# The MLP's transposed rows and relu rows begin at other places within 256 bytes of SBUF

## The chip, the cores and the metric

One core of one Trainium2 chip. The metric is the device time of one execution in microseconds (us); lower is better. A change under 0.2% (about 2.1 us) can't be told from no change with runs of this kernel.

## The reference

Attention with random features (FAVOR), then layer normalisation and an MLP with a residual. Batch 8, 8 heads, 576 positions, head width 64, 128 features; the MLP is 512 -> 2048 -> 512, over 8 * 576 = 4608 rows, all in float32.

```python
q_s, k_s = q * scale, k * scale            # scale = 1 / sqrt(sqrt(64))
def phi(x):
    h = x @ omega.T - sum(x * x) / 2
    return exp(h - max(h)) / sqrt(m)
q_p, k_p = phi(q_s), phi(k_s)
num = q_p @ (k_p.T @ v);  den = q_p @ sum(k_p) + 1e-06
x   = num / den                            # to 8 x 576 x 512
xn  = (x - mean) / sqrt(var + 1e-06) * g_ln
out = x + relu(xn @ w_ch1) @ w_ch2
```

## The kernel before

The 4608 rows of the MLP are cut into nine tiles `t` of T = 512 rows, and the 2048 inner columns into 16 slices `f` of 128. A planner (`Plan`) runs all parts of the work as generators and writes down, in the order in which they come due by its costs, the instructions of each engine; what it fixes is an order for each engine, not times. The MLP's matmuls (`gen_mlp`) are the work of lowest rank that is always there: they stand in the TensorE's order in a fixed sequence, mm1(t, f) and then mm2 of the slice before, and the attention's small matmuls (L480, L510, L582, L583, L671, L755) are put between them where they come due.

Every product of the MLP is made of three matmuls in the type float32r (a float32 that the array takes in one pass at less precision), since each factor is split in a high part and the low part that remains: high by high, low weights by high rows, high weights by low rows.

- `gen_xnT1` (L755 to L761): four 128x128 transposes of one 128-row piece of the normalised rows go to a PSUM bank. ScalarE copies the bank to the high part of the tile `xnT` (L759), VectorE writes the rest to the low part (L761). `xnT` is one tile of 128 partitions x (2 parts, NK = 4 pieces of the inner dimension, 512 rows); there is one buffer of it.
- `mm1` (L782 to L784): for each of the four pieces k, the weights `w` of w_ch1 (128 columns of them) are the stationary operand and the 512 elements of row `xnT[:, part, k]` are the moving operand. The sum stands in a PSUM bank `b`.
- `relu` (L793, L795): ScalarE writes the high part of relu to the tile `hid`, VectorE the low part; `hid` is 128 partitions x (2 parts, 512), in two buffers, hid0 and hid1.
- `mm2` (L815 to L817): for each of four groups of 128 rows, 128 elements of `hid` are the stationary operand and 512 elements of the weights of w_ch2 the moving one. They add up over the 16 slices in four PSUM banks.

So `xnT` is read by matmuls (moving) and `hid` by weight loads (stationary, LDWEIGHTS). The weights `w1`, `w2` stay in SBUF for the whole run, 4096 bytes in each partition for a slice: 512 high, then 512 low elements.

In the built program all tiles of weights, `xnT`, both `hid`, `wide`, `kp` and `x` begin at a multiple of 256 bytes within a partition, and each row of 512 elements is 2048 bytes long. So every row that a matmul of the MLP streams, and every group of 128 elements that it loads as weights, begins at byte 0 of 256. The attention's `v` tiles don't: they have 65 elements for each head (260 bytes), and the three buffers begin at byte 128 (v0), 32 (v1) and 96 (v2) of 256.

Of the kernel before, what the change touches and what calls it, by code (L numbers as in the profile page):

```python
# [14 lines left out]
F32R = mybir.dt.float32r  # L15
U32 = mybir.dt.uint32
AF = mybir.ActivationFunctionType
ALU = mybir.AluOpType
# [4 lines left out]
P = 128  # L23
# [5 lines left out]
NK = DM // P  # L29
NF = DFF // P  # L30
# [5 lines left out]
T = 512  # L36
# [32 lines left out]
class Plan:  # L69
# [73 lines left out]
    def free(self, *names):  # L143
        for n in names:
            assert n not in self.places, n
            self.places[n] = self.cur.seen()
            self.cur.holds -= n[0] == "b" and 0 < self.cur.holds
            self.wake(lambda w: w[0] == "get" and n in w[1])

    def done(self, key):  # L150
        self.made[key] = self.cur.seen()
        self.wake(lambda w: w == ("wait", key))
# [38 lines left out]
def favor_ffn(ctx, tc, kT, kTr, vF, vR, qT, qD, omT, gT, w1, w2, out):  # L191
# [12 lines left out]
    nc = tc.nc  # L204
# [8 lines left out]
    def f32(ap):  # L213
        return ap.bitcast(F32)

    def act(n, k=1, c=0.09):
        return "run", {ACT: k * (c + 0.00084 * n)}

    def dve(n, k=1, c=0.065):
        return "run", {DVE: k * (c + 0.00105 * n)}  # L220

    def us(eng, t):
        return "run", {eng: t}
# [16 lines left out]
    def wait(*key):  # L240
        return "wait", key

    def names(tag, n):
        return plan.own(*(f"{tag}{i}" for i in range(n)))

    def tile_of(tag, shape, dtype=F32, pool=None):
        pool = pool or (wp if tag[1].isdigit() and tag[0] == "w" else small if tag[0:2] in ("kv", "mb", "st") or tag[0] == "v" else sb)
        return pool.tile(shape, dtype, tag=tag, name=tag, bufs=1)
# [6 lines left out]
    def bank(tag, n=512):  # L255
        return tile_of(tag, [P, 512], F32, ps)[:, 0:n]
# [5 lines left out]
    n_hid, n_xnT, n_mb, n_st = names("hid", 2), names("xnT", 1), names("mb", 3), names("st", 6)  # L262
# [6 lines left out]
    def at_now():  # L269
        return b_at if mlp_on else banks  # L270
# [118 lines left out]
    kvs, phis, xs, xnTs, pvs, pvt = {}, {}, {}, {}, {}, {}  # L389
# [341 lines left out]
    def gen_xnT():  # L731
        for c in range(NC):
            t, i = divmod(c, TC)
            plan.cur.rank = URGENT + t
            yield wait("x", c)
            xn_turn = yield "get", turn["xn"]
            t_n = yield "get", n_big
            _, x, mu, rs = xs[c]
            xn = tile_of(t_n, [P, DM])
            yield us(DVE, 0.34)  # L740
            nc.vector.tensor_scalar(out=xn, in0=x, scalar1=mu, scalar2=rs, op0=ALU.subtract, op1=ALU.mult)
            done(("xn", c))
            if i == 0:
                t_t = yield "get", n_xnT
                xnTs[t] = t_t, tile_of(t_t, [P, 2, NK, T], F32R)
            plan.add(plan.cur.rank, gen_xnT1(t, i, xn, t_n, xn_turn))

    def gen_xnT1(t, i, xn, t_n, xn_turn):
        xnT = xnTs[t][1]
        yield wait("ident")  # L750
        t_b = yield "get", at_now()
        yield us(PE, 0.46)
        pt = bank(t_b).rearrange("p (a b) -> p a b", b=P)
        for k in range(NK):
            nc.tensor.transpose(pt[:, k], xn[:, k * P : (k + 1) * P], ident)  # L755
        free(t_n, xn_turn)
        cols = slice(i * P, (i + 1) * P)
        yield us(ACT, 0.5)
        nc.scalar.copy(out=xnT[:, 0, :, cols], in_=pt)  # L759
        yield dve(DM)  # L760
        nc.vector.tensor_tensor(out=xnT[:, 1, :, cols], in0=pt, in1=f32(xnT[:, 0, :, cols]), op=ALU.subtract)  # L761
        free(t_b)
        done(("xnT", t, i))

# [3 lines left out]
    def mm1(t, f):  # L768
        for k in range(NK):
            yield wait("w", 1, f // NK * NK + k)  # L770
        for i in range(TC):
            yield wait("xnT", t, i)
        if not mlp_on:
            mlp_on.append(True)
        t_x, xnT = xnTs[t]
        t_b = yield "get", b_h
        ph = bank(t_b)
        for k in range(NK):
            yield us(PE, 3 * 0.225)
            w = wparts[1, f // NK * NK + k]  # L780
            cs = slice(f % NK * P, (f % NK + 1) * P)
            nc.tensor.matmul(ph, w[:, 0, cs], xnT[:, 0, k], start=(k == 0), stop=False)  # L782
            nc.tensor.matmul(ph, w[:, 1, cs], xnT[:, 0, k], start=False, stop=False)  # L783
            nc.tensor.matmul(ph, w[:, 0, cs], xnT[:, 1, k], start=False, stop=(k == NK - 1))  # L784
        if f == NF - 1:
            free(t_x)
        plan.add(MOST_URGENT, relu(t, f, t_b, ph))

    def relu(t, f, t_b, ph):
        t_h = yield "get", n_hid  # L790
        hl = tile_of(t_h, [P, 2, T], F32R)
        yield act(T, 1, 0.05)
        nc.scalar.activation(out=hl[:, 0], in_=ph, func=AF.Relu)  # L793
        yield dve(T)
        nc.vector.scalar_tensor_tensor(  # L795
            out=hl[:, 1], in0=ph, scalar=0.0, in1=f32(hl[:, 0]), op0=ALU.max, op1=ALU.subtract
        )
        free(t_b)
        hid[t, f] = t_h, hl
        done(("hid", t, f))  # L800

    accs = {}

    def mm2(t, f):
        yield wait("w", 2, f)
        yield wait("hid", t, f)
        t_h, hl = hid[t, f]
        w = wparts[2, f]
        for i in range(TC):
            if f == 0:  # L810
                t_b = yield "get", (b_acc[i],)
                accs[i] = bank(t_b)
            yield us(PE, 3 * 0.225)
            cs = slice(i * P, (i + 1) * P)
            nc.tensor.matmul(accs[i], hl[:, 0, cs], w[:, 0], start=(f == 0), stop=False)  # L815
            nc.tensor.matmul(accs[i], hl[:, 0, cs], w[:, 1], start=False, stop=False)  # L816
            nc.tensor.matmul(accs[i], hl[:, 1, cs], w[:, 0], start=False, stop=(f == NF - 1))  # L817
            if f == NF - 1:
                plan.add(MOST_URGENT, result(t, i, accs[i]))
        free(t_h)  # L820

    def result(t, i, acc):
        c = t * TC + i
        t_x, x = xs[c][0:2]
        yield dve(DM)
        nc.vector.tensor_tensor(out=x, in0=acc, in1=x, op=ALU.add)  # L826
        free(b_acc[i])
        yield dma(P * DM)
        nc.sync.dma_start(out[c * P : (c + 1) * P], x)
        free(t_x)  # L830
# [11 lines left out]
    def gen_mlp():  # L842
        last = None
        for t in range(NT):
            for f in range(NF):
                if f == 0 and last:
                    yield from mm2(*last)
                    last = None
                yield from mm1(t, f)
                if last:  # L850
                    yield from mm2(*last)
                last = t, f
        yield from mm2(*last)
# [14 lines left out]
    plan.add(RK, gen_keys())  # L868
    plan.add(RQ, gen_queries())
    plan.add(URGENT, gen_xnT())  # L870
    for b in range(B):
        plan.add(0, gen_kvfree(b))
# [54 lines left out]
```

## Time and profile before

| | |
|---|---|
| median of three runs | 1043.0 us (1042.22 to 1043.11) |
| the profiled execution: span from first to last instruction | 1040.8 us |
| the profiled execution's own device time | not given apart from the span; the span is 2.2 us under the median of the runs |
| granted TensorE clock | 1.000 |
| TensorE matmul, busy | 1032.0 us (99%), 5778 instructions |
| weight loads, busy | 863.4 us (83%) |
| VectorE / ScalarE / GpSimd, busy | 498.3 (48%) / 357.1 (34%) / 133.5 us (13%) |
| MLP matmuls (L782 to L784, L815 to L817) | 6 x 576 = 3456 |

A matmul's busy time in the profile is the time from its start to its modelled end, and neighbours overlap in the array: how fast the array takes matmuls is read from the distance between two starts, not from the mean duration. "PEld" is the weight load, which runs beside the matmul before it.

### The profile page before, as it was taken

Reading aid. Unit: us, or ns where it says so; the run is one execution under the profiler, and the core shown is the slowest. Engines: PE = TensorE matmul, PEld = TensorE weight load, DVE = VectorE, ACT = ScalarE, POOL = GpSimd, SP = SyncE. Lnnn points to the kernel's source line nnn. Section 1 sums busy time; section 2 is a strip of 40 time slices with the busy share of each in tenths; the row PEclk is TensorE's granted clock in tenths of the full one; section 3 lists DMA queues with packets and bytes.
Section 4 is the critical chain, followed back from the end, with each engine's and each line's share of the span. In section 5 each row is a group of like instructions: output and inputs, shape, how many; then the busy total and the mean of one; then the engine's idle time right before and its main releaser. Section 6 shows DMA issues by size and latency. Waiting matters only on the chain.

```text
span 1040.8 us, 14483 instructions
## 1 busy us (share of the span) xinstructions
PE 1032.0 (99%) x5778; PEld 863.4 (83%) x5778; DVE 498.3 (48%) x1045; ACT 357.1 (34%) x810; POOL 133.5 (13%) x80
## 2 busy tenths in 40 slices
PE   9999999999999999999999999999999999999998
PEld 7888888888887888888887888888878888888886
DVE  6999878366347521663147422751274134113112
ACT  7699746335334421253025421241133111102100
POOL 6000424014002300050002200140022000000000
PEclk9999999999999999999999999999999999999999
DMA  9564222121213100420032100200030010001001
GB/s 358 213 195 150 82 82 91 62 72 51 73 43 130 42 11 1 143 61 1 1 99 85 41 1 1 102 21 1 1 122 1 0 41 1 1 1 42 1 1 41
DMA packets 30308, 64.08 MB, mean 62 GB/s; under 512 B 3488, under 2 KB 3616, under 8 KB 30240
## 3 DMA queue, kind: packets, MB, share of 16 engines
q1 hardware_dynamic: 30240, 63.14, 17.9%
q8 instruction: 46, 0.75, 0.3%
q14 instruction: 22, 0.18, 0.1%
HBM read 53.69 MB, written 9.44 MB: 61 GB/s over the span
## 4 chain that ended last, share of the span: by engine, by line
PE 93%; DVE 4%; DMA 2%; SPq 1%; issue 1%; ACT 0%; ACTq 0%
PE b L815 13%; PE b L782 13%; PE b L784 12%; PE b L817 12%; PE b L816 12%; PE b L783 12%; PE b L480 5%; PE b L671 5%; PE b L510 3%; PE b L582 1%; PE b L583 1%; PE b L755 1%; DMA w<-w 1%; DVE x L826 1%; DMA w<-vF 0%
## 5 line engine op out<-in xcount | busy, mean ns | idle before, releaser
L795 DVE SCALAR_TENSOR_TENSOR hid<-b,hid 128x512 fp32r<-128x512 f32 x144 | 99.3, 689 | 382.5 <-ACT hid L793 381.9
L793 ACT ACTIVATE hid<-b 128x512 fp32r<-128x512 f32 x144 | 86.3, 599 | 445.8 <-PE b L784 445.4
L815 PE MATMUL b<-w,hid 128*128 128x512 f32 x576 | 231.6, 402 | 0.0
L782 PE MATMUL b<-xnT,w 128*128 128x512 f32 x576 | 230.4, 400 | 0.0
L817 PE MATMUL b<-w,hid 128*128 128x512 f32 x576 | 225.2, 391 | 0.0
L784 PE MATMUL b<-xnT,w 128*128 128x512 f32 x576 | 225.0, 391 | 0.1
L816 PE MATMUL b<-w,hid 128*128 128x512 f32 x576 | 224.9, 390 | 0.0
L783 PE MATMUL b<-xnT,w 128*128 128x512 f32 x576 | 224.5, 390 | 0.0
L604 POOL PARTITION_ALL_REDUCE wide<-wide x72 | 132.4, 1877 | 658.2 <-ACT st L713 268.3
L784 PEld LDWEIGHTS b<-xnT,w 128*128 128x128 f32 x576 | 108.2, 188 | 23.6 <-DVE xnT L761 0.5
L817 PEld LDWEIGHTS b<-w,hid 128*128 128x128 f32 x576 | 108.2, 188 | 23.0
L815 PEld LDWEIGHTS b<-w,hid 128*128 128x128 f32 x576 | 108.4, 188 | 22.6
L782 PEld LDWEIGHTS b<-xnT,w 128*128 128x128 f32 x576 | 108.4, 188 | 21.8
L783 PEld LDWEIGHTS b<-xnT,w 128*128 128x128 f32 x576 | 108.4, 188 | 20.6
L816 PEld LDWEIGHTS b<-w,hid 128*128 128x128 f32 x576 | 108.5, 188 | 20.3
L448 ACT ACTIVATE kp<-b,mb 128x128 f32<-128x128 f32 x272 | 75.3, 388 | 51.4 <-DVE mb L442 51.4
L671 PEld LDWEIGHTS b<-kv,wide 128*128 128x128 f32 (+1 forms) x640 | 67.2, 181 | 6.9 <-issue 2.8
L607 DVE TENSOR_TENSOR wide<-wide,wide 128x512 f32<-128x512 f32 x72 | 65.1, 909 | 13.3 <-POOL wide L604 12.8
L480 PEld LDWEIGHTS b<-v,kp 128*128 128x128 f32 (+1 forms) x576 | 64.2, 191 | 6.5 <-issue 1.6
L671 PE MATMUL b<-kv,wide 128*128 128x65 f32 (+1 forms) x640 | 66.8, 261 | 2.3 <-DVE st L678 1.2
L480 PE MATMUL b<-v,kp 128*128 128x65 f32 (+1 forms) x576 | 64.0, 272 | 0.0
L442 DVE TENSOR_REDUCE mb<-b 128x4 f32<-128x512 f32 x72 | 46.6, 681 | 30.9 <-PE b L510 30.8
(71 smaller groups left out, 800.0 us busy)
## 6 DMA issues: line engine op xcount, KB each, us to landing
w<-w SPq DMA_DIRECT2D x32, 512.0 KB, 8.9
wide<-qD SPq DMA_DIRECT2D x64, 256.0 KB, 2.7
out<-x SPq DMA_DIRECT2D x36, 256.0 KB, 2.0
v<-vF SPq DMA_DIRECT2D x28, 260.0 KB, 2.9
wide<-kT SPq DMA_DIRECT2D x28, 256.0 KB, 2.7
w<-vF SPq DMA_DIRECT2D x4, 260.0 KB, 4.8
v<-vR SPq DMA_DIRECT2D x4, 260.0 KB, 4.0
w<-kT SPq DMA_DIRECT2D x4, 256.0 KB, 4.8
```

What stands on the lines that cost most here:

```text
L448: nc.scalar.activation(out=kp[:, j], in_=pk[:, i], func=AF.Exp, scale=1.0, bias=mb[:, j : j + 1])
L480: nc.tensor.matmul(o[:, i], kp[r, slot(h)], v[r, h], start=(n > 0 or c + i == 0), stop=(n > 0 or (c == NFULL and i == 3)),)
L604: nc.gpsimd.partition_all_reduce(mx, qc, P, bass_isa.ReduceOp.max)
L671: nc.tensor.matmul(pn[a:z, i], phi(blk, h, slice(cols + a, cols + z)), kvs[b][1][:, h], start=True, stop=True)
L782: nc.tensor.matmul(ph, w[:, 0, cs], xnT[:, 0, k], start=(k == 0), stop=False)
L783: nc.tensor.matmul(ph, w[:, 1, cs], xnT[:, 0, k], start=False, stop=False)
L784: nc.tensor.matmul(ph, w[:, 0, cs], xnT[:, 1, k], start=False, stop=(k == NK - 1))
L793: nc.scalar.activation(out=hl[:, 0], in_=ph, func=AF.Relu)
L795: nc.vector.scalar_tensor_tensor(out=hl[:, 1], in0=ph, scalar=0.0, in1=f32(hl[:, 0]), op0=ALU.max, op1=ALU.subtract)
L815: nc.tensor.matmul(accs[i], hl[:, 0, cs], w[:, 0], start=(f == 0), stop=False)
L816: nc.tensor.matmul(accs[i], hl[:, 0, cs], w[:, 1], start=False, stop=False)
L817: nc.tensor.matmul(accs[i], hl[:, 1, cs], w[:, 0], start=False, stop=(f == NF - 1))
```

## The change

The tiles `xnT`, `hid0` and `hid1` become 64 elements (256 bytes) longer, and their rows are laid with gaps: a high row of `xnT` every 516 elements, a low row every 520, after the high ones; the two rows of `hid` begin at elements 8 and 528 in hid0, at 32 and 560 in hid1. All instructions stay the same in kind, number, order, size and waits on every engine: the two programs' orders differ in source lines alone. Since three tiles are longer by 256 bytes, the tiles that lie behind them in SBUF move by 256, 512 or 768 bytes; all keep their place within 256. The weights don't move at all.

The places at which rows begin, in bytes within 256, by the built programs:

| rows | read as | before | after |
|---|---|---|---|
| `xnT` high, k = 0, 1, 2, 3 | moving (L782, L783) | 0, 0, 0, 0 | 0, 16, 32, 48 |
| `xnT` low, k = 0, 1, 2, 3 | moving (L784) | 0, 0, 0, 0 | 64, 96, 128, 160 |
| `hid0` high, low | weight load (L815 and L816, L817) | 0, 0 | 32, 64 |
| `hid1` high, low | weight load (L815 and L816, L817) | 0, 0 | 128, 192 |
| weights `w1`, `w2` | weight load in mm1, moving in mm2 | 0 | 0 |

These are twelve rows at nine different places (32, 64 and 128 stand twice, once for an `xnT` row and once for a `hid` row).

```diff
             if i == 0:
                 t_t = yield "get", n_xnT
-                xnTs[t] = t_t, tile_of(t_t, [P, 2, NK, T], F32R)
+                u = tile_of(t_t, [P, 2 * NK * T + 64], F32R)
+                lo = NK * (T + 4)
+                xnTs[t] = t_t, (
+                    u[:, 0:lo].rearrange("p (a b) -> p a b", b=T + 4)[:, :, 0:T],
+                    u[:, lo : lo + NK * (T + 8)].rearrange("p (a b) -> p a b", b=T + 8)[:, :, 0:T],
+                )
...
-        nc.scalar.copy(out=xnT[:, 0, :, cols], in_=pt)
+        nc.scalar.copy(out=xnT[0][:, :, cols], in_=pt)
...
-            nc.tensor.matmul(ph, w[:, 0, cs], xnT[:, 0, k], start=(k == 0), stop=False)
+            nc.tensor.matmul(ph, w[:, 0, cs], xnT[0][:, k], start=(k == 0), stop=False)
...
-        hl = tile_of(t_h, [P, 2, T], F32R)
+        u = tile_of(t_h, [P, 2 * T + 64], F32R)
+        hl = [u[:, a : a + T] for a in ((8, T + 16), (32, T + 48))[n_hid.index(t_h)]]
...
-            nc.tensor.matmul(accs[i], hl[:, 0, cs], w[:, 0], start=(f == 0), stop=False)
+            nc.tensor.matmul(accs[i], hl[0][:, cs], w[:, 0], start=(f == 0), stop=False)
```

The other lines of the change write the same operands in the same way.

More of the change, by code (lines that the diff above doesn't have):

```diff
@@ L758, in gen_xnT1 @@
         yield us(ACT, 0.5)
-        nc.scalar.copy(out=xnT[:, 0, :, cols], in_=pt)
+        nc.scalar.copy(out=xnT[0][:, :, cols], in_=pt)
         yield dve(DM)
-        nc.vector.tensor_tensor(out=xnT[:, 1, :, cols], in0=pt, in1=f32(xnT[:, 0, :, cols]), op=ALU.subtract)
+        nc.vector.tensor_tensor(out=xnT[1][:, :, cols], in0=pt, in1=f32(xnT[0][:, :, cols]), op=ALU.subtract)
         free(t_b)
@@ L781, in mm1 @@
             cs = slice(f % NK * P, (f % NK + 1) * P)
-            nc.tensor.matmul(ph, w[:, 0, cs], xnT[:, 0, k], start=(k == 0), stop=False)
-            nc.tensor.matmul(ph, w[:, 1, cs], xnT[:, 0, k], start=False, stop=False)
-            nc.tensor.matmul(ph, w[:, 0, cs], xnT[:, 1, k], start=False, stop=(k == NK - 1))
+            nc.tensor.matmul(ph, w[:, 0, cs], xnT[0][:, k], start=(k == 0), stop=False)
+            nc.tensor.matmul(ph, w[:, 1, cs], xnT[0][:, k], start=False, stop=False)
+            nc.tensor.matmul(ph, w[:, 0, cs], xnT[1][:, k], start=False, stop=(k == NK - 1))
         if f == NF - 1:
@@ L790, in relu @@
         t_h = yield "get", n_hid
-        hl = tile_of(t_h, [P, 2, T], F32R)
+        u = tile_of(t_h, [P, 2 * T + 64], F32R)
+        hl = [u[:, a : a + T] for a in ((8, T + 16), (32, T + 48))[n_hid.index(t_h)]]
         yield act(T, 1, 0.05)
-        nc.scalar.activation(out=hl[:, 0], in_=ph, func=AF.Relu)
+        nc.scalar.activation(out=hl[0], in_=ph, func=AF.Relu)
         yield dve(T)
         nc.vector.scalar_tensor_tensor(
-            out=hl[:, 1], in0=ph, scalar=0.0, in1=f32(hl[:, 0]), op0=ALU.max, op1=ALU.subtract
+            out=hl[1], in0=ph, scalar=0.0, in1=f32(hl[0]), op0=ALU.max, op1=ALU.subtract
         )
@@ L814, in mm2 @@
             cs = slice(i * P, (i + 1) * P)
-            nc.tensor.matmul(accs[i], hl[:, 0, cs], w[:, 0], start=(f == 0), stop=False)
-            nc.tensor.matmul(accs[i], hl[:, 0, cs], w[:, 1], start=False, stop=False)
-            nc.tensor.matmul(accs[i], hl[:, 1, cs], w[:, 0], start=False, stop=(f == NF - 1))
+            nc.tensor.matmul(accs[i], hl[0][:, cs], w[:, 0], start=(f == 0), stop=False)
+            nc.tensor.matmul(accs[i], hl[0][:, cs], w[:, 1], start=False, stop=False)
+            nc.tensor.matmul(accs[i], hl[1][:, cs], w[:, 0], start=False, stop=(f == NF - 1))
             if f == NF - 1:
```

## The prediction

> **What bounds the kernel now.** I read the page's first part and its costliest groups, then the timeline of TensorE in a stretch that is all MLP.
>
> ```profile
> span 1040.8 us, 14483 instructions
> PE 1032.0 (99%) x5778; PEld 863.4 (83%) x5778; DVE 498.3 (48%) x1045; ACT 357.1 (34%) x810; POOL 133.5 (13%) x80
> ...
> L815 PE MATMUL b<-w,hid 128*128 128x512 f32 x576 | 231.6, 402 | 0.0
> L782 PE MATMUL b<-xnT,w 128*128 128x512 f32 x576 | 230.4, 400 | 0.0
> L817 PE MATMUL b<-w,hid 128*128 128x512 f32 x576 | 225.2, 391 | 0.0
> L784 PE MATMUL b<-xnT,w 128*128 128x512 f32 x576 | 225.0, 391 | 0.1
> L816 PE MATMUL b<-w,hid 128*128 128x512 f32 x576 | 224.9, 390 | 0.0
> L783 PE MATMUL b<-xnT,w 128*128 128x512 f32 x576 | 224.5, 390 | 0.0
> ...
> L784 PEld LDWEIGHTS b<-xnT,w 128*128 128x128 f32 x576 | 108.2, 188 | 23.6 <-DVE xnT L761 0.5
> L817 PEld LDWEIGHTS b<-w,hid 128*128 128x128 f32 x576 | 108.2, 188 | 23.0
> ```
>
> TensorE is busy for 1032.0 of 1040.8 us, and its six MLP lines show no idle time ahead of them (the last column, 0.0 or 0.1). So the pace at which the array takes these 3456 matmuls sets the time. That pace stands in the timeline of the MLP alone (start, duration):
>
> ```profile
> 499.70 0.39 PE L815 MATMUL b<-w,hid 128*128 128x512 f32 x1
> ...
> 500.83 0.39 PE L817 MATMUL b<-w,hid 128*128 128x512 f32 x1
> 500.83 0.19 PEld L782 LDWEIGHTS b<-xnT,w 128*128 128x128 f32 x1
> 501.06 0.39 PE L782 MATMUL b<-xnT,w 128*128 128x512 f32 x1
> 501.06 0.19 PEld L783 LDWEIGHTS b<-xnT,w 128*128 128x128 f32 x1
> ...
> 503.55 0.39 PE L784 MATMUL b<-xnT,w 128*128 128x512 f32 x1
> ```
>
> From 499.70 to 503.55 there are 17 steps from start to start: 3.85 / 17 = 0.2265 us. Over 3456 matmuls that is 783 us, 75% of the span. In each step the weights of the next matmul are loaded: the load starts with the matmul and takes 0.188 us, so it is over 38 ns before its matmul can start. The moving stream sets the pace, not the load. Both kinds of step (mm1, whose moving row is `xnT`, and mm2, whose loaded weights are `hid`) have the same pace.
>
> Is there anything in that pace to be had? The warming matmuls (L308, 256 columns in bf16, a weight load with each) give a comparison:
>
> ```profile
> 37.61 0.27 PE L308 MATMUL b<-spin 128*128 128x256 bf16 x1
> 38.11 5.08 PE L308 MATMUL b<-spin 128*128 128x256 bf16 x45
> ```
>
> Less the last one's own 0.27 us, 44 steps take 4.81 us: 109.3 ns for 256 columns, 218.6 ns for twice as many. The MLP's 226.5 ns for 512 float32r columns is 7.9 ns above that. 7.9 ns x 3456 = 27 us is what the place of the rows could be worth at the very most by these rows, if all of the excess came from rows and weights that begin at the same place; nothing in the trace says that it does. The Trainium skill, "TensorE: Matmul & The Clock Gate", section "Back-to-back issue gap", gives a gap of about 216 ns for 512 columns at the full clock. This trace disagrees by 11 ns, and by that figure the most to be had would be an estimated 37 us instead of 27.
>
> **The change part by part.** It adds and removes no instruction and moves none, so there are four costs to find: the moving reads of `xnT`, the weight loads of `hid`, the writes to both, and the tiles behind them.
>
> (1) The moving reads in mm1, 1728 matmuls. Does the place of a moving row, or its distance to the weights that are loaded beside it, change the pace? All MLP rows of before begin at byte 0, so no row shows another place at this speed. The nearest are the matmuls of keys by values: float32 in two slower passes, 65 columns, moving from `v` and loading from `kp`, which begins at 0. The built program tells which buffer each of these pieces reads: one that begins at 96 (v2, at 259.48), 32 (v1, at 364.03) and 128 (v0, at 379.83). Each head is 260 bytes on, so that most of them are not even at a multiple of 16:
>
> ```profile
> 259.48 1.89 PE L480 MATMUL b<-v,kp 128*128 128x65 f32 x16
> 364.03 1.89 PE L480 MATMUL b<-v,kp 128*128 128x65 f32 x16
> 379.83 1.89 PE L480 MATMUL b<-v,kp 128*128 128x65 f32 x16
> ...
> L480 PE MATMUL b<-v,kp x576: 217/275/325, 26.2 to 612.2; 128*128 128x65 f32 x149, 64*128 64x65 f32 x43
> ```
>
> Sixteen take 1.89 us from each place: 0.01 us of resolution over 15 steps is 0.7 ns a step. So neither the place itself nor the distance between the two reads (96, 32, 128) costs or saves 0.7 ns there. What the row can't show is the float32r stream, which takes a column in 0.44 ns (226.5 / 512), and those are passes that the weight load paces, at 108 ns (1.89 less a last one of 0.27, the median 275 ns, by 15). Bounds for (1): from above, one more 64-byte piece per row that doesn't begin at a multiple of 64 (a row of 2048 bytes is 32 such pieces; 226.5 / 32 = 7.1 ns). Those rows are k = 1, 2, 3 of the high part, each used in two matmuls, and k = 1, 3 of the low: 8 of 12 matmuls, 1152 in all, +8.2 us. From below, -7.9 ns for each low row, which begins in another 64-byte quarter than the weights: 576 matmuls, -4.6 us. I take 0, by the row of L480, the only one that reads from different places.
>
> (2) The weight loads of `hid` in mm2, 1728 of them. A longer load is covered by the 38 ns between its end and the next matmul; even a tenth more of 188 ns is 19 ns and costs nothing. If that cover were gone, each ns would cost 1.7 us. If moving reads and weight loads get in each other's way, all these loads begin in another quarter than the weights that stream at the same time, or half way through one (32): -7.9 ns x 1728 = -13.7 us as the lower bound; the upper is 0. I take 0, since by the same three rows of L480 distance alone changed nothing.
>
> (3) The writes. ScalarE and VectorE write the same sizes; in `xnT` the four pieces were a stride of 512 elements apart and are now 516 or 520 apart.
>
> ```profile
> L759 ACT CAST xnT<-b x36: 567/587/593, 44.3 to 947.3; 128x512 fp32r<-128x512 f32 x36
> L761 DVE TENSOR_TENSOR xnT<-b,xnT x36: 678/680/693, 45.1 to 948.6; 128x512 fp32r<-128x512 f32 x36
> ...
> L793 ACT ACTIVATE hid<-b x144: 575/598/654, 52.8 to 1031.6; 128x512 fp32r<-128x512 f32 x144
> L795 DVE SCALAR_TENSOR_TENSOR hid<-b,hid x144: 672/691/693, 54.0 to 1032.3; 128x512 fp32r<-128x512 f32 x144
> ```
>
> The relu pair takes 0.598 + 0.691 = 1.29 us after mm1 of its slice, and between that and its mm2 stand the 12 matmuls of the slice before, 12 x 0.2265 = 2.72 us. 1.4 us of cover less the hand-overs, and the matmul rows above have 0.0 of idle time. At a change of tile the four pieces of `xnT` must be there: the last low part of all starts at 948.6 and ends at 949.3, and its mm1 starts here:
>
> ```profile
> 949.61 0.39 PE L817 MATMUL b<-w,hid 128*128 128x512 f32 x1
> 949.84 0.39 PE L782 MATMUL b<-xnT,w 128*128 128x512 f32 x1
> ```
>
> 0.5 us later, one normal step after the matmul ahead. Were each of four writes 10% slower (0.07 us), that would be 0.28 us, and still be covered. Without cover: nine tiles x 0.28 = 2.5 us, the upper bound; 0 below. I take 0.
>
> (4) The tiles behind move by multiples of 256 bytes. Nothing in the trace has a price for that; the `wide` and `x` tiles stand at many multiples of 256 already. 0.
>
> Sum: 0 + 0 + 0 + 0. The span stays at 1040.8 us, and the forecast is the runs' median, 1043.0 us, 2.2 us above that span. With the bounds: -18.3 us (4.6 + 13.7) and +10.7 us (8.2 + 2.5).
>
> **The rivals.**
>
> *A: the two reads of TensorE do get in each other's way, and the change frees them (faster).* For it: at float32r's speed the step is 7.9 ns above twice the warming matmul's, every row and every weight of before begins at byte 0, and here the moving stream is what paces, unlike in L480. It would take the excess from the 576 low-row matmuls of mm1 and the 1728 of mm2: 2304 x 7.9 = 18.2 us, so 1024.8 us; a share of that if only some distances help (half: 1033.9 us). It counts from 0.6 ns a matmul (2.1 us / 3456). Against it: the stream runs through 2048 bytes in 226 ns while a load goes through 512 in 188 ns, so whatever the distance at the start, the one overtakes the other and passes through all distances within 256 bytes in each step; the start only says when. On this point the Trainium skill, "SBUF — State Buffer", section "Who interferes with whom", says that TensorE has two independent read ports, one for the moving operand and one for the weights, and that it waits on no one. By that rule the places change nothing and the time is 1043.0; the equal rows of L480 agree with it, at their speed.
>
> *B: a moving row off a 64-byte multiple pays for one more piece (slower).* 1152 matmuls x 7.1 ns = 8.2 us, 1051.2 us. It decides from 1.8 ns for each of these (2.1 us / 1152). For it: at 0.44 ns a column the stream has no room to hide a piece more. Against it: in L480 the starts are at 4-byte steps and nothing shows; there, though, the load paces, so that a small cost could hide. If the piece costs only the one column time of 0.44 ns, it is 0.5 us and not to be seen. The same page of the Trainium skill, section "Door 1: The DMA port swizzle", gives SBUF lines of 16 bytes; all new places are multiples of 16, so by that there is no extra line and B gives 1043.0 too.
>
> *C: nothing changes.* This is the forecast.
>
> **How the numbers follow.** C 0.57: the one line that reads from three places shows no difference, and a load and a stream pass through all distances anyhow. A 0.25, of which some 0.12 at 1024.8 or below and the rest up to 1040: there is an excess that the trace doesn't explain, and no row at this speed speaks against A. B 0.18, mostly from 1045 to 1051, with the writes of (3) in it. "Same" means within 0.2%, about 2.1 us, which is what a measurement can tell. The range from 1029 to 1051.5 leaves out the strong half of A and little of B; the likeliest case's own range is 1041.5 to 1044.5.
>
> **What would show it.** In the timeline of the changed kernel, 17 steps between L815 and L784 in a stretch of MLP should again take 3.85 us. Were A right, the steps of mm2 and those of the low rows would be near 219 ns and the high rows' unchanged, so mm1 and mm2 would differ. Were B right, mm1's steps would be near 231 to 234 ns, and mm2's at 226.5. The weight loads of L815 to L817 tell whether (2) grew: 188 ns before, and nothing follows up to 226. L759 and L761 should stay at 587 and 680 ns, and L793 and L795 at 598 and 691. What would make this wrong is a pace of the float32r stream that depends on place or distance, which no row of before can show.

## The result and the profile after

The change makes the kernel slower: 1057.37 us median (1057.26 to 1057.79), against 1043.05 us of before beside it, a ratio of 1.0137 (95% interval 1.0123 to 1.0152). That is 14.3 us more; the forecast was no change, 1043.0 us with a range up to 1051.5.

The page's first part and costliest groups, after:

```profile
span 1055.5 us, 14483 instructions
PE 1046.7 (99%) x5778; PEld 864.0 (82%) x5778; DVE 499.4 (47%) x1045; ACT 357.7 (34%) x810; POOL 133.4 (13%) x80
...
L821 PE MATMUL b<-w,hid 128*128 128x512 f32 x576 | 234.4, 407 | 0.0
L787 PE MATMUL b<-xnT,w 128*128 128x512 f32 x576 | 232.5, 404 | 0.0
L789 PE MATMUL b<-xnT,w 128*128 128x512 f32 x576 | 227.0, 394 | 0.1
L823 PE MATMUL b<-w,hid 128*128 128x512 f32 x576 | 226.9, 394 | 0.0
L788 PE MATMUL b<-xnT,w 128*128 128x512 f32 x576 | 226.7, 394 | 0.0
L822 PE MATMUL b<-w,hid 128*128 128x512 f32 x576 | 226.6, 393 | 0.0
...
L823 PEld LDWEIGHTS b<-w,hid 128*128 128x128 f32 x576 | 108.2, 188 | 25.7
```

The whole loss is in TensorE's busy time: 1046.7 - 1032.0 = 14.7 us, as much as the span grew (1055.5 - 1040.8). Shared among the 3456 matmuls of the MLP that is 4.25 ns for each. By their busy times the three lines of mm1 (L787 to L789) have 6.3 us more than before and the three of mm2 (L821 to L823) 6.2 us, so both have about equal parts. The weight loads (PEld) still take 188 ns. The writes did not change either; by the tile `xnT`:

```profile
L764 ACT CAST xnT<-b x36: 568/587/593, 44.6 to 960.0; 128x512 fp32r<-128x512 f32 x36
L766 DVE TENSOR_TENSOR xnT<-b,xnT x36: 681/683/692, 45.4 to 961.3; 128x512 fp32r<-128x512 f32 x36
```

In the timeline of the MLP alone the distance from start to start has grown:

```profile
507.74 0.39 PE L788 MATMUL b<-xnT,w 128*128 128x512 f32 x1
...
509.13 0.39 PE L822 MATMUL b<-w,hid 128*128 128x512 f32 x1
509.13 0.19 PEld L823 LDWEIGHTS b<-w,hid 128*128 128x128 f32 x1
509.36 0.39 PE L823 MATMUL b<-w,hid 128*128 128x512 f32 x1
...
511.68 0.40 PE L787 MATMUL b<-xnT,w 128*128 128x512 f32 x1
```

17 steps take 3.94 us, 231.8 ns each; it was 226.5. These 5.3 ns are more than the 4.25 ns of the average, since the steps fewer than twelve behind an attention matmul, which were slow before too, grew by about 2 ns only. The load at 509.13 ends at 509.32, some 40 ns ahead of its matmul's start at 509.36: as before, no matmul waits for its weights by this profile. The stream itself has become slower.

### The profile page after: what moved, and what is told of

Read it like the earlier page. It is cut to its first block, busy times and chain, and to the rows that moved or that the text cites. A ratio compares the mean times of both kernels' runs of the same rounds, so it can differ in the third digit from the quotient of the medians.

```text
span 1055.5 us, 14483 instructions
## 1 busy us (share of the span) xinstructions
PE 1046.7 (99%) x5778; PEld 864.0 (82%) x5778; DVE 499.4 (47%) x1045; ACT 357.7 (34%) x810; POOL 133.4 (13%) x80
## 4 chain that ended last, share of the span: by engine, by line
PE 94%; DVE 5%; issue 1%; ACT 0%; POOL 0%; ACTq 0%
PE b L821 13%; PE b L787 13%; PE b L789 13%; PE b L788 13%; PE b L823 13%; PE b L822 12%; PE b L480 5%; PE b L671 5%; PE b L510 3%; PE b L582 1%; PE b L583 1%; PE b L760 1%; DVE wide L607 1%; DVE x L682 0%; PE b L308 0%
## 5 line engine op out<-in xcount | busy, mean ns | idle before, releaser
L821 PE MATMUL b<-w,hid 128*128 128x512 f32 x576 | 234.4, 407 | 0.0
L787 PE MATMUL b<-xnT,w 128*128 128x512 f32 x576 | 232.5, 404 | 0.0
L789 PE MATMUL b<-xnT,w 128*128 128x512 f32 x576 | 227.0, 394 | 0.1
L823 PE MATMUL b<-w,hid 128*128 128x512 f32 x576 | 226.9, 394 | 0.0
L788 PE MATMUL b<-xnT,w 128*128 128x512 f32 x576 | 226.7, 394 | 0.0
L822 PE MATMUL b<-w,hid 128*128 128x512 f32 x576 | 226.6, 393 | 0.0
L789 PEld LDWEIGHTS b<-xnT,w 128*128 128x128 f32 x576 | 108.2, 188 | 25.9 <-DVE xnT L766 0.5
L823 PEld LDWEIGHTS b<-w,hid 128*128 128x128 f32 x576 | 108.2, 188 | 25.7
L821 PEld LDWEIGHTS b<-w,hid 128*128 128x128 f32 x576 | 108.4, 188 | 24.6
L787 PEld LDWEIGHTS b<-xnT,w 128*128 128x128 f32 x576 | 108.3, 188 | 23.9
L480 PEld LDWEIGHTS b<-v,kp 128*128 128x128 f32 (+1 forms) x576 | 64.2, 190 | 6.6 <-issue 2.0
L480 PE MATMUL b<-v,kp 128*128 128x65 f32 (+1 forms) x576 | 64.0, 272 | 0.0
```

The lines of the kernel that those rows point to most:

```text
L480: nc.tensor.matmul(o[:, i], kp[r, slot(h)], v[r, h], start=(n > 0 or c + i == 0), stop=(n > 0 or (c == NFULL and i == 3)),)
L787: nc.tensor.matmul(ph, w[:, 0, cs], xnT[0][:, k], start=(k == 0), stop=False)
L788: nc.tensor.matmul(ph, w[:, 1, cs], xnT[0][:, k], start=False, stop=False)
L789: nc.tensor.matmul(ph, w[:, 0, cs], xnT[1][:, k], start=False, stop=(k == NK - 1))
L821: nc.tensor.matmul(accs[i], hl[0][:, cs], w[:, 0], start=(f == 0), stop=False)
L822: nc.tensor.matmul(accs[i], hl[0][:, cs], w[:, 1], start=False, stop=False)
```

## The experiments

The theory after the result: TensorE's two reads, the moving row and the weights loaded beside it for the next matmul, get in each other's way depending on the distance of their places within 256 bytes (D). Its rivals: the place of a row itself (P), the shift of the tiles that lie behind (R), the change of place from one matmul to the next (M). `xn_rows(a)` below stands for rows of `xnT` without gaps from element `a` on.

| run | what differs from before | median us | ratio to before (95% interval) |
|---|---|---|---|
| e1 | tiles 256 bytes longer, rows at 0 | 1043.22 | 1.000 (0.9991 to 1.0010) |
| e2 | hid rows at the new places | 1056.23 | 1.0126 (1.0111 to 1.0141) |
| e3 | all tiles 32 bytes on | 1043.12 | 1.000 (0.9990 to 1.0009) |
| e4 | one place for each 512-row tile | 1058.05 | one run |
| e5 | xnT rows at the new places | 1052.91 | 1.0092 (1.0077 to 1.0107) |
| e6 | hid rows at the new places in 3 of 16 slices | 1045.85 | 1.0026 (1.0016 to 1.0035) |
| e7 | one place for each 512-row tile, others | 1058.16 | one run |
| e8 | 3 of 12 loads of an mm1 have 64 of 128 columns | 1048.10 | one run |
| e9 | hid, xnT and 4 of 16 slices of w2 at 64 | 1054.78 | 1.0112 (1.0095 to 1.0128) |
| e10 | mm2 streams 384 columns | 966.38 | one run |
| e11 | mm2 loads 64 columns | 1044.09 | one run |

**Padding alone (e1).**

```diff
+                u = tile_of(t_t, [P, 2 * NK * T + 64], F32R)
+                xnTs[t] = t_t, xn_rows(0)
...
+        u = tile_of(t_h, [P, 2 * T + 64], F32R)
+        hl = [u[:, a : a + T] for a in (0, 0 + T)]
```

> The three tiles are 256 bytes longer, as in the change, but all rows begin at byte 0 of 256 again, so only the tiles behind them stand elsewhere. Theory D (distance): TensorE's two reads get in each other's way when the moving row and the weights loaded beside it begin at different places within 256 bytes; then this is as before, 1043 us and 226.5 ns from start to start. Theory P (place): a row that doesn't begin at a certain multiple costs by itself; as before too. Theory R (relocation): the shift of the other tiles by 256 to 768 bytes makes the loss; then 1057 us and about 231 ns a step.

1043.22 us. R falls: the loss is not from the tiles behind. Here xnT lies 256 and hid1 512 bytes further on than before, so distances that are a multiple of 256 cost nothing either.

**All tiles 32 bytes on (e3).**

```diff
+    const.tile([P, 8], F32, name="gap")
     spin = const.tile([P, 2 * P], BF16, name="spin")
```

> The kernel before with one unused tile of 32 bytes ahead of all others: each tile, the weights too, begins 32 bytes further on, so all MLP rows and weights begin at byte 32 and the distance between moving row and weights is 0 as before. Theory D: 1043 us, 226.5 ns a step. Theory P: every row is off a multiple of 64, so all 3456 steps lose, 1050 to 1065 us. Theory R: anything over 1043 us.

1043.12 us, and 17 steps take 3.85 us as before:

```profile
499.79 0.39 PE L816 MATMUL b<-w,hid 128*128 128x512 f32 x1
...
503.64 0.39 PE L785 MATMUL b<-xnT,w 128*128 128x512 f32 x1
```

No row begins at a multiple of 64 here, and nothing is lost. P falls for this place, and with it the prediction's rival B: by this run what counts is not the place but the distance to the other read.

**The relu's rows alone (e2) and the transposed rows alone (e5).** e2 has e1's `xn_rows(0)` and the change's places in hid; e5 has the change's places in xnT and hid at `(0, 0 + T)`.

> Only the relu's rows stand at their new places (32, 64, 128, 192); the transposed rows are back at byte 0. Theory D: the 1728 steps of mm2 are slower by 4 to 5 ns, those of mm1 stay at 226.5 ns, so about half of the loss, 1050 us. Theory P in its form of the prediction's rival (a moving row off a multiple pays for a piece more): weight loads have 38 ns of cover, so nothing is lost, 1043 us. Theory R: 1057 us.

> The complement of the run with the relu's rows alone: only the transposed rows stand at their new places, hid is back at byte 0. Theory D with a carry-over (a step that was disturbed leaves the two reads out of step for some eight steps, even where all places are equal again): mm1 about 231.5 ns, mm2 some 229 to 230 ns although all its places are 0, in all 1053 to 1056 us, so the two halves don't add up to the whole. Theory D without a carry-over: mm1 slow, mm2 at 226.5 ns, 1050 us. If the hid rows alone matter: 1044 us.

e2: +13.1 us, more than the 7 us that D as stated there gave. e5: +10.0 us against its own runs of before (1042.92 us), just under the 1053 to 1056 us of D with a carry-over. Together 23.1 us against 14.3 us of both at once: the two halves don't add up. The timelines say why. In e2 a whole mm2 with moved loads, and behind it an mm1 whose moving rows and weights are all at 0:

```profile
1005.93 0.40 PE L820 MATMUL b<-w,hid 128*128 128x512 f32 x1
...
1008.74 0.40 PE L786 MATMUL b<-xnT,w 128*128 128x512 f32 x1
...
1010.59 0.39 PE L788 MATMUL b<-xnT,w 128*128 128x512 f32 x1
```

The twelve steps of mm2 take 2.81 us, 234 ns each. The eight behind them take 1.85 us, 231 ns each, with nothing moved in them. And in e5 an mm2 with all places at 0, after an mm1 with moved rows:

```profile
1013.28 0.39 PE L821 MATMUL b<-w,hid 128*128 128x512 f32 x1
...
1014.44 0.39 PE L823 MATMUL b<-w,hid 128*128 128x512 f32 x1
...
1016.03 0.39 PE L787 MATMUL b<-xnT,w 128*128 128x512 f32 x1
```

The first five steps take 1.16 us (232 ns each), the other seven 1.59 us (227 ns each). A disturbance outlasts its cause by five to eight matmuls. So each half also slows matmuls of the other half. Averaged over all steps that stand at least twelve behind an attention matmul, which no longer disturbs them, mm1 is at 230.3 ns in e2 and mm2 at 228.6 ns in e5 (226.7 and 226.6 before). In the change itself, mm1 is at 231.8 and mm2 at 231.7 ns, no more than its own half alone gives (mm1 231.9 in e5, mm2 232.8 in e2). The sum of the two runs counts the loss of many steps twice. e2 shows one more thing: every moving row is at 0 there, and the place of the loads alone slows the stream.

**The relu's rows in three slices of sixteen (e6).** To see the carry-over by itself.

```diff
-        hl = [u[:, a : a + T] for a in ((8, T + 16), (32, T + 48))[n_hid.index(t_h)]]
+        hl = [u[:, a : a + T] for a in (((8, T + 16), (32, T + 48))[n_hid.index(t_h)] if f % 5 == 1 else (0, T))]
```

> The relu's rows stand at their new places in the slices f = 1, 6 and 11 of 16 alone (27 of 144 slices), all else at byte 0. Theory D with a carry-over: the 12 steps of such a slice at about 232 ns, the first eight or so of the 12 mm1 steps behind it at about 231 ns though all their places are equal, then 226.5 ns up to the next; 27 x (66 + 40 ns) = 2.9 us, 1046 us. Without a carry-over: 27 x 66 ns = 1.8 us, 1044.9 us, and the mm1 steps behind at 226.5 ns.

1045.85 us, 2.9 us more than its own runs of before (1042.92), as forecast with a carry-over; by the interval of the ratio 1.7 us is still possible, so the time alone doesn't decide. The timeline does. From a moved mm2 through the mm1 behind it into the next mm2:

```profile
1017.59 0.40 PE L820 MATMUL b<-w,hid 128*128 128x512 f32 x1
...
1020.39 0.40 PE L786 MATMUL b<-xnT,w 128*128 128x512 f32 x1
...
1022.24 0.39 PE L788 MATMUL b<-xnT,w 128*128 128x512 f32 x1
...
1025.87 0.39 PE L786 MATMUL b<-xnT,w 128*128 128x512 f32 x1
```

The twelve steps of the moved mm2 take 2.80 us (233 ns), then come eight with all places equal in 1.85 us (231 ns), then sixteen in 3.63 us (227 ns). Behind the moved slices of the other tiles it is the same by the averages: slow for some eight steps, then 227 ns.

**One place for each tile of 512 rows (e4, e7).**

```diff
+                xnTs[t] = t_t, xn_rows((0, 4, 8, 16, 24, 32, 48, 56, 60)[t])
...
+        hl = [u[:, a : a + T] for a in (p, p + T)]     # p: the same place of tile t
```

> All rows of xnT and hid of one 512-row tile begin at the same place, another one for each of the nine tiles: 0, 16, 32, 64, 96, 128, 192, 224, 240 bytes; the weights stay at 0. Read tile by tile in the timeline. Theory D: the tile at 0 runs at 226.5 ns a step, the other eight at some 228 to 236 ns by their distance, mm1 and mm2 both. Theory P: tiles at 64, 128, 192 run at 226.5 ns and those at 16, 32, 96, 224 and 240 slower, in mm1 alone. Theory M (mixture: what costs is that the place changes from one matmul to the next): mm1 runs at 226.5 ns in every tile, since there the place is the same from row to row.

> As the run by tile, at other places: 0, 4, 8, 16, 48, 80, 112, 160, 208 bytes. Theory D: the tile at 0 at 226.5 ns; those at 4 and 8 still there if a difference inside one 16-byte line does nothing, else slower; all others 228 to 234 ns. If a distance existed at which the reads miss each other altogether, its tile would be under 226.5 ns, as some single steps of the changed kernel are (224 to 225 ns).

In e4, mm1 of the tile at 0, of the tile at 64 and of the tile at 240 bytes, and mm2 of that last one:

```profile
110.88 0.39 PE L786 MATMUL b<-xnT,w 128*128 128x512 f32 x1
...
113.60 0.39 PE L820 MATMUL b<-w,hid 128*128 128x512 f32 x1
...
500.35 0.40 PE L786 MATMUL b<-xnT,w 128*128 128x512 f32 x1
...
503.14 0.39 PE L820 MATMUL b<-w,hid 128*128 128x512 f32 x1
...
1016.32 0.40 PE L786 MATMUL b<-xnT,w 128*128 128x512 f32 x1
...
1019.12 0.39 PE L820 MATMUL b<-w,hid 128*128 128x512 f32 x1
...
1020.28 0.39 PE L822 MATMUL b<-w,hid 128*128 128x512 f32 x1
...
1021.64 0.39 PE L822 MATMUL b<-w,hid 128*128 128x512 f32 x1
```

Twelve steps take 2.72 us at 0 (227 ns), 2.79 us at 64 (233 ns) and 2.80 us at 240 (233 ns). M falls: within each mm1 the place never changes, and it stays slow to the end. 64 is a multiple of 64 and as slow as the others. One combination besides 0 does come back: in mm2 of the last tile, with the stream at 0 and the load at 240, five steps take 1.16 us (232 ns) and the next six 1.36 us (227 ns). The mm1 before it, with stream and load the other way round, does not. Averaged over the steps that stand at least twelve behind an attention matmul, the eight tiles that are not at 0 have mm1 at 231 to 234 ns and mm2 at 229 to 234 ns; the lowest of these are the mm2 at 240 and at 192.

e7 adds 4, 8, 48, 80, 112, 160 and 208 bytes. A difference of 4 bytes is enough, and so is one of 8, with 2.84 and 2.81 us for the twelve steps of an mm1 (237 and 234 ns; the first of the two begins six matmuls behind an attention matmul, since the tile at 4 has few longer stretches):

```profile
181.24 0.40 PE L786 MATMUL b<-xnT,w 128*128 128x512 f32 x1
...
184.08 0.40 PE L820 MATMUL b<-w,hid 128*128 128x512 f32 x1
...
414.55 0.39 PE L786 MATMUL b<-xnT,w 128*128 128x512 f32 x1
...
417.36 0.39 PE L820 MATMUL b<-w,hid 128*128 128x512 f32 x1
```

Averaged as above, the tiles of e7 that are not at 0 have mm1 at 231 to 237 and mm2 at 230 to 234 ns. No place in either run settles below 226.5 ns.

**Loads of half the columns in one product (e8) and in mm2 (e11), fewer columns to stream (e10).** What does the load cost when all places are equal?

```diff
# e8
-            nc.tensor.matmul(ph, w[:, 0, cs], xnT[:, 1, k], start=False, stop=(k == NK - 1))
+            n = P if k == NK - 1 else 64
+            nc.tensor.matmul(ph[0:n], w[:, 0, f % NK * P : f % NK * P + n], xnT[:, 1, k], start=False, stop=(k == NK - 1))
# e10, and so the other two matmuls of mm2; Q = 384
+            nc.tensor.matmul(accs[i][:, 0:Q], hl[:, 0, cs], w[:, 0, 0:Q], start=(f == 0), stop=False)
# e11, Q = 64
+            cs = slice(i * P, i * P + Q)
+            nc.tensor.matmul(accs[i][0:Q], hl[:, 0, cs], w[:, 0], start=(f == 0), stop=False)
```

> All places as before. The third product of mm1 (low rows) is made with 64 of 128 columns of weights for k = 0, 1, 2, so that half the output rows lack that part; the weight load ahead of it is half as long. If the weight load takes cycles from the moving stream beside it (theory D's ground): the step in which the half load runs (that of the second product, 226.5 ns before) falls, by half of its excess over 512 columns, to some 220 ns. If the excess is the stream's own: 226.5 ns still.

> All places as before. The matmuls of mm2 stream 384 of 512 columns; the last quarter of the output columns lacks the MLP's part. What is the 226.5 ns step made of? If the excess over the stream belongs to the weight load (the load takes cycles, once for each 16 bytes of 128 weights): 384 columns at full speed 160 ns and the same 13 ns on top, 173 ns in settled steps. If it belongs to the stream, one part in 16: 170 ns. If it is a fixed 2.7 ns for a matmul with the rest in proportion: 171 ns.

> All places as before. The matmuls of mm2 load 64 of 128 weight columns, so half of the output rows lack the MLP's part; all loads within mm2 are half as long, in a regular row. If the load takes the cycles from the stream: about 220 ns in settled steps of mm2. If the excess is the stream's own: 226.5 ns.

e10, an mm2 of 384 columns from its seventh matmul on, and the mm1 of 512 columns behind it:

```profile
932.99 0.33 PE L816 MATMUL b<-w,hid 128*128 128x384 f32 x1
...
934.03 0.39 PE L783 MATMUL b<-xnT,w 128*128 128x512 f32 x1
...
936.11 0.39 PE L783 MATMUL b<-xnT,w 128*128 128x512 f32 x1
...
936.79 0.33 PE L816 MATMUL b<-w,hid 128*128 128x384 f32 x1
```

Six steps of mm2 in 1.04 us, 173.3 ns; the average of 69 such stretches is 173.4 ns. With 226.5 ns for 512 columns, 128 columns are worth 53.2 ns, 0.416 ns a column, and 512 of them 213 ns: by these two points the remaining 13 to 14 ns belong to the matmul with its load, not to the columns. So the first of the three expectations held in size. The mm1 behind shows something that no expectation had: its first nine steps take 2.08 us (231 ns), the last three 0.68 us (227 ns), though all places are equal. So a stream of another length throws the pace off too.

That the load's reads take the 13 to 14 ns is not shown: a load of half the columns should then have lowered the step. It didn't. e11, a whole mm2 with loads of 64 columns, and the line of these loads on the page:

```profile
1005.45 0.40 PE L816 MATMUL b<-w,hid 128*64 128x512 f32 x1
...
1008.21 0.39 PE L783 MATMUL b<-xnT,w 128*128 128x512 f32 x1
...
L817 PEld LDWEIGHTS b<-w,hid 128*64 128x64 f32 x576 | 77.6, 135 | 46.9
```

2.76 us for twelve steps, 230 ns, slower than with whole loads. A load of half the columns takes 135 ns, 72% of 188. The kernel as a whole is only 0.8 us above its runs of before (1043.30), which can't be told from no change: the mm2 steps at least twelve behind an attention matmul take 209.7 us in all against 206.5, but those nearer behind one take 169.0 against 171.7. e8 became 5.2 us slower in its one run. A whole mm1 of it:

```profile
1006.77 0.39 PE L782 MATMUL b<-xnT,w 128*128 128x512 f32 x1
...
1009.52 0.39 PE L816 MATMUL b<-w,hid 128*128 128x512 f32 x1
```

Twelve steps in 2.75 us, 229 ns. The steps beside the shorter loads don't fall to 220 ns: for k = 0, 1, 2 they stand at 225, 228 and 236 ns on average. Shorter loads with equal places disturb the pace too; in both runs the expectations of 220 or 226.5 ns missed.

**One unused tile between the weights (e9).** Equal places in hid and xnT for all slices, but the weights of w_ch2 at two places.

```diff
+        if (n, f) == (2, 8):
+            wp.tile([P, 16], F32, name="gap")
         r = tile_of(tag, [P, DM, 2], U32)
```

> The kernel before with one unused tile of 64 bytes between the weights: hid, xnT, wide, x and the weights of w_ch2 for f = 8 to 11 begin at byte 64, all other weights at byte 0. Theory D: mm2 of f = 8 to 11 has the distance 0 at place 64 and comes back, after the carry-over of some eight steps from mm1, to 226.5 ns a step; mm2 of the other twelve f and all of mm1 have the distance 64 and stay at 231 to 234 ns; in all some 1058 us. Theory P (the place of the rows of xnT and hid itself): all f alike. If nothing but the gaps between rows mattered: 1043 us.

1054.78 us, some 3 us under the 1058 that D gave. In the eighth tile of 512 rows, mm2 of f = 10 (weights at 64, like hid) and of f = 12 (weights at 0):

```profile
930.70 0.39 PE L817 MATMUL b<-w,hid 128*128 128x512 f32 x1
...
933.42 0.39 PE L784 MATMUL b<-xnT,w 128*128 128x512 f32 x1
...
941.63 0.39 PE L817 MATMUL b<-w,hid 128*128 128x512 f32 x1
...
944.43 0.40 PE L784 MATMUL b<-xnT,w 128*128 128x512 f32 x1
```

2.72 us against 2.80 us for the twelve steps, 227 and 233 ns, with hid at 64 in both. This is D within one program: the rows stand at the same place, and only the distance to the other read differs. f = 10 is at 227 ns from its first step, without the carry-over that was expected from mm1, so a disturbance doesn't always carry over; mm1 with a distance of 64 stood at 229 to 233 ns, by slice, and not at the 231 to 234 ns expected.

## Why the prediction was wrong

**What bounds the kernel** held: TensorE's pace on 3456 matmuls sets the time, before and after.

**Step (1), the moving reads, taken at 0**, failed. The row chosen for it was L480, where three places took the same 1.89 us. The text noted that those passes are paced by the load at 108 ns and stream at a slower rate, and used them all the same as the only row with different places. They say nothing of the fast stream, and there the loss was. e5 measured the step at +10.0 us on its own, with the mm2 steps that it slows by carry-over, beyond its upper bound of 8.2.

**Step (2), the weight loads, taken at 0 with an upper bound of 0**, failed worst: +13.1 us in e2, with the mm1 steps that it slows by carry-over. The step asked only whether the load would end late, and covered it by 38 ns. The load does not end late, at 188 ns still; its place slows the stream of the matmul beside it all the same. A cover against a late end is none against a slower neighbour.

**Step (3), the writes, and step (4), the tiles behind**, held: the durations are 587 and 683 ns, and e1 is at 1.000.

**Rival A** came nearest in mechanism, with the two reads in each other's way, which the runs fit without showing it; its sign was wrong: it took equal places for the bad case, and they are the best that the runs found. Its counter-argument, that a load and a stream pass through all distances in each step, so that the start only says when, is refuted by e4 and e9: with another distance at the start the pace is slower for as long as that distance stays. The start is not all that counts, though: e8, e10 and e11 have slow steps at equal places.

**Rival B** had the right sign by the wrong cause: 1152 moving rows off a multiple of 64. e3 has all of them off and loses nothing; 64 in e4 is on and loses 6 ns a step. The sign given for B, mm1 at 231 to 234 ns and mm2 at 226.5, came true in its first half alone: in the change both are at 232 ns.

The Trainium skill, "SBUF — State Buffer", section "Who interferes with whom", says that TensorE has two independent read ports, one for the moving operand and one for the weights, and that it waits on no one. The runs differ, and they decide: in e2 the place of the loads alone takes the steps of mm2 from 226.5 to 234 ns, in the rows shown.

The trace of before did hold a sign that went unread. After most of the attention's matmuls between the MLP's, the pace is off for some steps, though all MLP places are equal. Behind sixteen of L510, by the timeline of before:

```profile
295.90 1.16 PE L510 MATMUL b<-om,wide 64*128 64x128 f32 x16
...
297.33 0.39 PE L783 MATMUL b<-xnT,w 128*128 128x512 f32 x1
...
298.49 0.39 PE L782 MATMUL b<-xnT,w 128*128 128x512 f32 x1
...
299.85 0.39 PE L815 MATMUL b<-w,hid 128*128 128x512 f32 x1
```

From 297.33 on, five steps take 1.16 us (232 ns), then six 1.36 us (227 ns). 227 ns is the settled pace of the whole case, and 232 ns is near the pace of the changed kernel. They showed that 226.5 ns is a pace into which the stream settles and out of which it can be thrown, so that a change of places had something to lose.

## What to carry to other kernels

Where float32r matmuls follow each other without a gap, let the moving rows and the weights that are loaded beside them begin at the same place within 256 bytes; other places for all the rows of `xnT`, of `hid` or of both cost 0.9 to 1.4% of the whole kernel here (e5, e2, the change). Look at the steps from start to start right behind a disturbance in the trace before: if they go through a slower stretch and come back, the steady pace is a state that can be lost. A row of another type or speed, paced by something else, is no evidence that an address is free.

## What the runs showed of the hardware

- The place of a weight load changes the pace of the matmul that streams beside it, though the load is over some 40 ns ahead of need. Equal places: 226.5 ns for 512 float32r columns; others, by the rows shown: 232 to 237 ns on average, for a difference of 4 bytes as well (e7).
- What counts is the distance within 256 bytes, not the place: all at 32 (e3) or load and stream at 64 (e9) are as good as 0; moving `xnT` by 256 and hid1 by 512 bytes (e1) costs nothing.
- After the cause is gone, the slower pace mostly lasts five to nine matmuls (e5, e6, e10); in e9 it did not carry over.
- The settled step is 0.416 ns a column and 13 to 14 ns beside, by two lengths, 384 and 512 columns (e10).
- Open: why equal places settle and others don't, why stream at 0 and load at 240 settle too (e4), and why loads of half the columns (e8, e11) or a stream of another length (e10), at equal places, make it slower. The runs fit a contention of the two reads, but none of them shows where in the chip it arises.
